# Local attention scores in 64 by 70 blocks instead of 36 by 42, with new settings for the planner that orders the work

## The chip, the cores and the metric

One core of a Trainium2 chip runs the whole program. The metric is the device time of one execution in microseconds, as the median of several runs; lower is better.

## The reference

Input: `q`, `k`, `v` of shape (4 batches, 8 heads, 576 positions, 64), and the weights of two feed-forward layers. Three things follow one another.

1. Attention, twice, for each batch and head. One branch averages `q`, `k` and `v` over groups of 4 positions, runs a full softmax attention over the 144 means, and repeats each result 4 times. The other, the local branch, takes at full resolution only keys with |i - j| < 4, so 7 keys for each query:

```python
mask = np.abs(pos[:, None] - pos[None, :]) < factor      # factor = 4
scores = np.where(mask, scale * np.matmul(q, k.transpose(0, 1, 3, 2)), -1e9)
out_local = np.matmul(softmax(scores), v)
x = (out_up + out_local)       # then (B, H, S, D) -> 2304 tokens x 512
```

2. Layer 1 on the 2304 tokens: `h = x @ w_in` (512 to 2048), `g = max(h, 0) + alpha * min(h, 0)`, `y = g @ w_out` (2048 to 512).
3. Layer 2 of the same sizes with an ELU between its two products.

## The kernel before

**Layer 1** is cut into 128 steps. A step is one group of 288 tokens and one slice `f` of 128 of the 2048 hidden columns: `mm_in` multiplies the tokens by the slice of `w_in`, `th_elem` applies the activation (ScalarE for the part below zero, VectorE for the sum), and, up to two steps later, `out1` multiplies by the slice of `w_out` into four accumulating PSUM banks. There are 8 groups, two to each batch. Operands are split into a high and a low part in the type fp32r, and each product is the sum of three matmuls (high by high, high by low, low by high). ScalarE makes the high part by a copy, VectorE the low part by a subtraction. **The first `F1` steps are different**: they work on the first group's first `F1` slices with unsplit fp32 operands, so that TensorE can start before any split is made; the hardware runs such a matmul as two passes, which appear as two instructions in the trace. Then come the 16 slices of the second group, then the rest of the first, then groups 2 to 7. A weight slice below `F1` is called late: it is decoded first, used unsplit, and split later by `th_late`, which needs one more ScalarE copy than the direct way in `th_conv`.

**Attention** is cut into threads (Python generators) that run beside layer 1. Batch 0 is done in the first 67 us, its local branch by `d_mm` in blocks of 64 queries by 70 keys. Batches 1 to 3 must each be ready before layer 1 reaches their groups at steps 32, 64 and 96. A thread `th_S(b, p)` makes the local scores of one pair of heads: `s_mm` multiplies blocks of 36 queries by 42 keys, `s_ev` copies them out of PSUM (ScalarE), `s_write` stores them to a scratch in DRAM, and `s_read` reads them back by a slanted pattern, 7 scores to a query. In `s_mm` one head lies on rows 0 to 63 of the array (`r = 0`) and the other on rows 64 to 127; the first half of the 576 positions (`c = 0`) goes to PSUM partitions 0 to 63 and the second half (`c = 1`) to those from 64 on, so four matmuls in a row use four different quadrants. `c = 0` is computed 64 queries wide though 36 are kept. Batch 1 makes both heads of its four pairs so, batches 2 and 3 half of theirs: eight `th_S` in all. The other heads of batches 2 and 3 get their scores on VectorE (`s_dve`). The product with the values (`av_ops`) shifts over 7 offsets; for the offsets listed in `AVA` ScalarE does the multiplication (`scale`), for the others VectorE.

**The order of work.** No order is written down by hand. While the program is built, a model of the chip (`_Clock`) keeps a time for each engine, and the order of instructions on each in-order queue comes out of it. A thread yields what it waits for: a key, a buffer token, an engine, or PSUM banks. Between the matmuls of layer 1, `tick` and `fill` let waiting threads emit their work: consumers when the model says that their data are there, TensorE jobs (those that wait for banks) by `pe(budget)` in order of priority until a budget of modelled TensorE time is used up. `PB` is that budget at a tick, `FB` at the start of a step and before `out1`, `RB` while layer 1 itself has to wait. Each thread has a priority (`P1`, `OS`, `OP`, `OSO`, `STEP` and others go into it), some a first step at which they may start (`OPS` for the loads of batches 2 and 3, `ST1` and `ST2` for batch 1), and a limit `LS` on how far ahead of TensorE an engine may be filled. If TensorE would otherwise fall idle, matmuls on a constant tile called `warm` are put in. What the chip then does differently from the model shows as waits in the trace, since the queues keep their order.

Of the kernel before, what the change touches and what calls it, by code (L numbers as in the profile page):

```python
# [7 lines left out]
F32 = mybir.dt.float32  # L8
# [10 lines left out]
S = 576  # L19
D = 64  # L20
NP = H // 2
# [5 lines left out]
NT = 18  # L27
# [1 line left out]
G1 = HT * CH  # L29
NG1 = 2 * B  # L30
NTOK = B * S
BLK = 36
WIN = 7
HALO = 3
KW = BLK + 2 * HALO
NU = 2 * S // BLK
SD = S // 4
TS = 3
LAG = 2
SP_ = S + 2 * HALO  # L40
F1 = 6
VK = 5
YS = 4
LORD = "q0 m q1 v0 d0 q2 v1 d1 q3 v2 d2 v3 d3"
# [2 lines left out]
VP = -15  # L47
DP = -14.5
NP0 = -14.95
STEP = 0.5  # L50
TC = 103
STG = ("n", "gh", "gl", "n", "gh", "gl")
G2 = 512
# [12 lines left out]
ECONV = 100.0  # L66
DLA = 2000.0
PB = 1000.0
FB = 300.0
RB = 300.0  # L70
PF = 5
CS = 6
OS = 4
OP = 13
OPS = -6
OSD = 4
OSO = 0
OAV = 12
OX = -5
UD = -9.5  # L80
# [5 lines left out]
ST2 = 3  # L86
OSS = 0
V1 = 3
LS = 800.0
PM = 300.0  # L90
DMG = 50.0
PM0 = 150.0
DMG0 = 400.0
GATE = "xc", 0, 0
AVA = {1: (2, 4, 6), 2: (2, 4, 6), 3: ()}
SDVE = {1: (), 2: (0,), 3: (0,)}
QUAD = {2, 3}
QORD = 0, 2, 1, 3
# [168 lines left out]
class _Engine:  # L267
# [3 lines left out]
    def cost(self, op, kw, args):  # L271
        if op == "transpose":
            return int(args[1].shape[0]) / 1.2 + 3, int(args[1].shape[0]) * int(args[0].shape[0]) / 16384
        if op == "matmul":
            n, m = _free(kw["out"]), int(kw["out"].shape[0])
            share = int(kw["lhsT"].shape[0]) * m / 16384
            if kw["lhsT"].dtype == BF16:
                return n / 2.4, share
            if kw["lhsT"].dtype == F32R:
                return max(n * 0.4375 + 7, m / 1.2 + 3), share  # L280
            if int(kw["lhsT"].shape[0]) == D and m == BLK:
                return 20.0, share
            if int(kw["lhsT"].shape[0]) == D and int(kw["lhsT"].offset) >= D * int(kw["lhsT"].ap[0][0]):
                return 8.0, share
            if m == D:
                second = int(kw["out"].offset) >= D * int(kw["out"].ap[0][0])
                return 36.0 if second else n * 4 / 2.4 + 16, share
            return n * 4 / 2.4 + 6, share
        sb = (kw["in_"] if "in_" in kw else kw["in0"]).space != bass.MemoryType.PSUM
        if self.name == "ACT":  # L290
            n = _free(kw["out"])
            return (93 if sb else 51) + n / 1.2 + 93.0 * sum(k in kw and not isinstance(kw[k], float) for k in ("scale", "bias")) \
                + (93.0 if "accum_out" in kw else 0.0), None
        n = _free(kw.get("in_", kw["out"]))
        if self.name == "POOL":
            return 150 + n * 2.25, None
        if op == "reciprocal":
            return 68 + n * 6.25, None
        fast = sb and op in ("tensor_scalar", "tensor_copy")
        ptr = op == "scalar_tensor_tensor" and not isinstance(kw["scalar"], (int, float))  # L300
        return 68 + n * (0.52 if fast else 1.0417) + (60 if ptr else 0), None
# [20 lines left out]
def fused_kernel(ctx: ExitStack, tc: tile.TileContext, qk, vt, vl, ql, kl, w_in1, w_out1, alpha,  # L322
# [3 lines left out]
    PE, ACT, DVE, SP, POOL = (_Engine(n, e, ck) for n, e in  # L326
                              (("PE", nc.tensor), ("ACT", nc.scalar), ("DVE", nc.vector), ("SP", nc.sync),
                               ("POOL", nc.gpsimd)))
# [3 lines left out]
    dram = ctx.enter_context(tc.tile_pool(name="dram", bufs=1, space=bass.MemoryType.DRAM))  # L332
# [17 lines left out]
    yT0 = dram.tile([DM, G1], F32, name="yT0a")  # L350
    xsp = dram.tile([128, KT, G1], F32, name="xsp")
    osp = dram.tile([NTOK, DM], F32, name="osp")
    scr = {(b, r): dram.tile([4 * NU // 2, BLK * (KW + 1)], F32, name=f"scr{b}_{r}")
           for b in range(1, B) for r in range(2) if r not in SDVE[b]}

    pB = tc.tile_pool(name="pB", bufs=1)
# [2 lines left out]
    Ap = pA.__enter__()  # L359
# [35 lines left out]

    late = [(1, nm, f) for f in range(F1) for nm in ("i", "o")]

# [183 lines left out]

    def s_mm(b, p, bks):
        t = st["qk", b, p]
        for i in range(NU // 4):
            for c in range(2):
                k = c * (NU // 4) + i
                w = BLK if c else D
                for r in range(2):
                    r0 = r * D
                    PE.matmul(out=bks[r][c * D:c * D + w, i * KW:(i + 1) * KW],  # L590
                              lhsT=t[0][r0:r0 + D, HALO + k * BLK:HALO + k * BLK + w],
                              rhs=t[1][r0:r0 + D, k * BLK:k * BLK + KW], start=True, stop=True)

    def s_ev(bks):
        t = Ap.tile([D + BLK, 2, NU // 4, KW], F32, tag="ss", name="ss", bufs=2)
        for r in range(2):
            ACT.activation(out=t[:, r], in_=bks[r][0:D + BLK, 0:NU // 4 * KW].rearrange("q (u k) -> q u k", k=KW),
                           func=AF.Copy)
        return t

    def s_write(b, p, t):
        for i in range(2):
            u0, r = p * (NU // 2), i
            if b in QUAD:
                u0, r = (2 * p + r - NP) * (NU // 2), 1
            for c in range(2):
                u1 = u0 + c * (NU // 4)
                SP.dma_start(out=scr[b, r][u1:u1 + NU // 4, 0:BLK * KW].rearrange("u (q k) -> q u k", k=KW),
                             in_=t[c * D:c * D + BLK, i])

    def band(t):
        return t.rearrange("u (j t x) -> (u j) t x", t=NT, x=KW + 1)[:, :, 0:WIN]

    def s_read(b):
        for r in (0, 1):
# [195 lines left out]
    T7 = NS1 - NF  # L811
    segs = [(1, 0, 0, F1, 0, 0), (1, 1, 0, NF, 0, 1), (1, 0, F1, NF, 0, 2)]
    segs += [(1, g, 0, NF, g // 2, g % 2) for g in range(2, NG1)]
# [236 lines left out]

    def th_qk(b, p):
        yield "key", "sq", b, p
        if b not in QUAD or p >= NP // 2:
            yield "key", "smm", b, p
        put("qk")

# [101 lines left out]
    def th_soft(b):  # L1158
        yield "key", "sal", b
        for r in range(2):  # L1160
            if r in SDVE[b]:
                for u in range(2):
                    for i in range(HT // TS):
                        yield "key", "SD", b, u, i, r
            else:
                for p in range(NP // 2 if b in QUAD else 0, NP):
                    yield "key", "S", b, p
        yield ("SP",)
        s_read(b)
        yield "tok", "a"  # L1170
        yield ("DVE",)
        softmax_a((b,))
        put("sd")
        yield ("ACT",)
        softmax_e((b,))
        yield ("DVE",)
        softmax_b((b,))
        finish("a", b)
# [230 lines left out]
    def th_elem(s, f):  # L1409
# [3 lines left out]
        n = pool.tile([128, n_], F32, tag="n", name="n", bufs=2)  # L1413
        if s < F1:
            r = pool.tile([128, n_], F32, tag="gh", name="r", bufs=3)
# [7 lines left out]
        finish("h", s)  # L1423
        if s < F1:
            gs[s] = (r, None)
# [11 lines left out]
    def out1(s):  # L1437
# [3 lines left out]
        gh, gl = gs.pop(s)  # L1441
        wk = ("w32" if s < F1 else "w", key)
        run_until(*wk)
# [3 lines left out]
        for m in range(KT):  # L1447
# [3 lines left out]
            at(*t)  # L1451
            if s < F1:
                PE.matmul(out=accb[m][:, :G1], lhsT=W32[key][:, m * 128:(m + 1) * 128], rhs=gh, start=first, stop=last)
# [340 lines left out]
    with tc.manual_schedule():  # L1794
# [4 lines left out]
        for step in LORD.split():  # L1799
            p = int(step[1:] or 0)  # L1800
# [16 lines left out]
        for p in range(NP):  # L1817
            spawn(th_pair(0, p), VP + p * STEP)
            spawn(th_da0(p), DP + p * STEP)
            spawn(th_dense(p, 0), NP0 + p * STEP)  # L1820
            spawn(th_dense(p, 1), US + p / 10, 0)
# [5 lines left out]
        for b in range(1, B):  # L1827
            g0 = 32 * (b - 1)
            for z in range(NP):
                p = QORD[z] if b in QUAD else z  # L1830
                if b not in QUAD or p >= NP // 2:
                    spawn(th_S(b, p), g0 + OS + z if b > 1 else P1 + z / 4)
                spawn(th_qk(b, p), -20)
                spawn(th_pair(b, p), g0 + OP + z if b > 1 else P1 + z / 4, g0 + 2 * z + OPS if b > 1 else ST1 + ST2 * z)
            if b in QUAD:
                for i in range(NP // 2):
                    spawn(th_dav(b, i), g0 + OP + 2 * i + 1)
            spawn(th_sal(b), g0)
            for u in range(2):
                for i in range(HT // TS):  # L1840
                    for r in SDVE[b]:
                        spawn(th_SD(b, u, i, r), g0 + OSD, g0 + OSS, LS)
            spawn(th_soft(b), g0 + OSO, g0)
            for u in range(2):
                spawn(th_vl(b, u), g0 + 5 + u)
                spawn(th_av(b, u), g0 + OAV + 16 * u, -1, LS)
                for i in range(HT // TS):
                    spawn(th_x(b, u, i), g0 + 16 * u + OX + i / 10)
        at(4000.0)
        DVE.tensor_scalar(out=nal, in0=nal, scalar1=-1.0, scalar2=1.0, op0=ALU.mult, op1=ALU.add)  # L1850
        for s in range(NS1):
            slot[0] = s if s else -1
            ly, g, f, first, last, i = seq[s]
# [3 lines left out]
            if s == TC:  # L1857
# [7 lines left out]
                for q in range(NQ):  # L1865
                    p = 2 + max(0, q - NJ + 1) + q / 100
# [13 lines left out]
            if s < F1:  # L1880
                t = 0.0
            else:
                run_until("xc", *segs[i][4:6])
                t = tm["x"]
# [30 lines left out]
        for u in range(NU2):  # L1915
            slot[0] = NS1 + u
            i, j = divmod(u, NJ)
# [106 lines left out]
```

## Time and profile before

| | us |
|---|---|
| median of 3 runs (lowest, highest) | 895.57 (894.94, 895.63) |
| the profiled execution | 896.16 |
| its span, from first to last instruction | 894.1 |
| TensorE matmul busy | 881.1 (99%), 6858 instructions |
| VectorE busy | 740.4 (83%) |
| ScalarE busy | 557.0 (62%) |
| share of TensorE in the chain that ended last | 87% |

A busy TensorE is not one at its peak: matmuls are pipelined, so one of 290 ns begins every 130 ns, and the record of the last before a wait hides a part of that wait. Throughput is therefore read from starts, and idle time from the idle column of a timeline. In timelines the columns are the start, the time from start to end, the engine, the source line, the operation, the tiles (out<-in), their shape and the count, and in brackets the idle time before, with what ended it. All operations pass through one helper, so the source line is the same for all; the tile names tell them apart: `bank<-qk` is `s_mm`, `bank<-qk,qk` is `d_mm`, `x,rawi` and `r,rawo` are the unsplit steps, `xh`, `xl`, `gh`, `gl` with `wi`, `wo` the split ones.

### The profile page before, as it was taken

Reading aid. Unit: us, or ns where it says so; the run is one execution under the profiler, and the core shown is the slowest. Engines: PE = TensorE matmul, PEld = TensorE weight load, DVE = VectorE, ACT = ScalarE, POOL = GpSimd, SP = SyncE. Lnnn points to the kernel's source line nnn. Section 1 sums busy time; section 2 is a strip of 40 time slices with the busy share of each in tenths; the row PEclk is TensorE's granted clock in tenths of the full one; section 3 lists DMA queues with packets and bytes.
Section 4 is the critical chain, followed back from the end, with each engine's and each line's share of the span. In section 5 each row is a group of like instructions: output and inputs, shape, how many; then the busy total and the mean of one; then the engine's idle time right before and its main releaser. Section 6 shows DMA issues by size and latency. Waiting matters only on the chain.

```text
span 894.1 us, 17959 instructions
## 1 busy us (share of the span) xinstructions
PE 881.1 (99%) x6858; PEld 817.1 (91%) x6858; DVE 740.4 (83%) x1600; ACT 557.0 (62%) x1488; POOL 0.2 (0%) x4
## 2 busy tenths in 40 slices
PE   8999999999999999999999999999999999999998
PEld 6678999999998999999999988889999989999987
DVE  5898999999797997997567899888797569888852
ACT  5899887894468844233355676656665457656643
POOL 0000000000000000000000000000000000000000
PEclk9999999999999999999999999999999999999999
DMA  9668733503405032013201733232404063251502
GB/s 293 227 216 284 238 64 108 169 28 101 126 9 169 28 98 57 1 46 111 105 28 59 241 105 121 96 111 79 160 31 164 1 215 117 97 180 33 189 22 73
DMA packets 68310, 102.80 MB, mean 115 GB/s; under 512 B 26704, under 2 KB 43344, under 8 KB 68224
## 3 DMA queue, kind: packets, MB, share of 16 engines
q1 hardware_dynamic: 68224, 101.65, 35.3%
q8 instruction: 54, 0.88, 0.4%
q14 instruction: 32, 0.26, 0.1%
HBM read 84.75 MB, written 16.88 MB: 114 GB/s over the span
## 4 chain that ended last, share of the span: by engine, by line
PE 87%; DVE 4%; ACT 4%; DMA 3%; issue 1%; SPq 0%; DVEq 0%
PE bank L317 87%; ACT n L317 1%; DMA qk<-in_qk_dram 1%; DMA vl<-in_vl_dram 1%; ACT dP L317 1%; DMA rawi<-in_w_in_dram 1%; DMA v<-in_vt_dram 1%; DVE qk L317 0%; ACT P L317 0%; SPq L317 0%; ACT xq L317 0%; DVE P L317 0%; DVE xq L317 0%; ACT gh L317 0%; DVE Dmx L317 0%
## 5 line engine op out<-in xcount | busy, mean ns | idle before, releaser
L317 PE MATMUL bank<-xh,wi 128*128 128x288 f32 x976 | 221.1, 299 | 0.2 <-ACT xh L317 0.2
L317 PE MATMUL bank<-gh,wo 128*128 128x288 f32 x976 | 219.6, 298 | 0.0
L317 PEld LDWEIGHTS bank<-xq,wi 128*128 128x128 f32 x1536 | 194.5, 191 | 6.4 <-DVE xq L317 0.3
L317 PE MATMUL bank<-xq,wi 128*128 128x256 f32 x1536 | 196.6, 283 | 0.1
L317 ACT ACTIVATE n<-bank 128x288 f32<-128x288 f32 (+1 forms) x176 | 70.4, 401 | 180.1 <-PE bank L317 176.7
L317 PE MATMUL bank<-wo,gh 128*128 128x512 f32 x576 | 179.1, 392 | 0.0
L317 PEld LDWEIGHTS bank<-xh,wi 128*128 128x128 f32 x976 | 164.3, 188 | 3.3 <-issue 2.3
L317 PEld LDWEIGHTS bank<-gh,wo 128*128 128x128 f32 x976 | 164.7, 188 | 1.6 <-issue 1.4
L317 PE MATMUL bank<-gl,wo 128*128 128x288 f32 x488 | 144.8, 297 | 0.9 <-DVE gl L317 0.9
L317 PE MATMUL bank<-xl,wi 128*128 128x288 f32 x488 | 143.8, 295 | 0.4 <-DVE xl L317 0.4
L317 PEld LDWEIGHTS bank<-wo,gh 128*128 128x128 f32 x576 | 103.1, 189 | 17.4
L317 PE MATMUL bank<-wo,gl 128*128 128x512 f32 x288 | 112.6, 391 | 0.2 <-DVE gl L317 0.2
L317 PEld LDWEIGHTS bank<-gl,wo 128*128 128x128 f32 x488 | 91.9, 188 | 1.3 <-DVE gl L317 1.3
L317 PEld LDWEIGHTS bank<-xl,wi 128*128 128x128 f32 x488 | 92.0, 189 | 1.0 <-DVE xl L317 0.9
L317 DVE SCALAR_TENSOR_TENSOR r<-n,nal,bank 128x288 f32<-128x288 f32 x128 | 65.1, 509 | 27.4 <-ACT n L317 26.9
L317 ACT ACTIVATE gh<-r 128x288 fp32r<-128x288 f32 x122 | 53.9, 442 | 53.5 <-DVE r L317 53.3
L317 PEld LDWEIGHTS bank<-wo,gl 128*128 128x128 f32 x288 | 54.1, 188 | 13.2 <-DVE gl L317 1.4
L317 DVE TENSOR_TENSOR gl<-r,gh 128x288 fp32r<-128x288 f32 x122 | 55.2, 453 | 11.1 <-ACT gh L317 10.2
L317 ACT ACTIVATE pa<-vl,a 128x64 f32<-128x64 f32 x216 | 55.4, 342 | 0.5 <-DVE a L317 0.5
L317 DVE TENSOR_TENSOR gl<-n,gh 128x512 fp32r<-128x512 f32 (+1 forms) x80 | 50.3, 633 | 6.1 <-ACT gh L317 5.1
L317 DVE TENSOR_TENSOR c<-m,bank 128x256 f32<-128x256 f32 x64 | 26.2, 417 | 33.4 <-PE bank L317 33.2
L317 ACT ACTIVATE gh<-n 128x512 fp32r<-128x512 f32 (+1 forms) x80 | 45.9, 581 | 11.3 <-DVE n L317 11.1
(121 smaller groups left out, 1239.7 us busy)
## 6 DMA issues: line engine op xcount, KB each, us to landing
rawo<-in_w_out_dram SPq DMA_DIRECT2D x38, 512.0 KB
rawi<-in_w_in_dram SPq DMA_DIRECT2D x36, 512.0 KB
qk<-in_qk_dram SPq DMA_DIRECT2D x12, 582.0 KB
vl<-in_vl_dram SPq DMA_DIRECT2D x6, 960.0 KB
x<-yT SPq DMA_DIRECT2D x8, 576.0 KB
osp<-os SPq DMA_DIRECT2D x18, 256.0 KB
os<-osp SPq DMA_DIRECT2D x18, 256.0 KB
out_dram<-os SPq DMA_DIRECT2D x18, 256.0 KB
```

The lines of the kernel that those rows point to most:

```text
L317: return fn(*args, **kw)
```

## The change

The block of local scores becomes 64 queries by 70 keys. 576 positions are 9 such blocks; each column half takes 5, so the middle one is computed in both halves, and the second half writes only its last 4. The settings of the planner are changed along with it, and so is the number of unsplit steps (`F1`, 6 to 8). The model's price of the score matmuls is set anew. Which heads are computed where (`SDVE`) is not changed.

```diff
-BLK = 36
+BLK = 64
-NU = 2 * S // BLK
+NU = S // BLK
+NC = (NU + 1) // 2
-F1 = 6
+F1 = 8
-STEP = 0.5
+STEP = 1.5
-FB = 300.0
-RB = 300.0
+FB = 200.0
+RB = 500.0
-OPS = -6
+OPS = -8
-OSO = 0
+OSO = -2
-LS = 800.0
+LS = 1200.0
-AVA = {1: (2, 4, 6), 2: (2, 4, 6), 3: ()}
+AVA = {1: (2, 4, 6), 2: (3, 5), 3: (3,)}
...
-            if int(kw["lhsT"].shape[0]) == D and m == BLK:
-                return 20.0, share
+            if str(getattr(kw["lhsT"].tensor, "tag", "")).startswith("qk_"):
+                first = [int(kw[k].offset) < D * int(kw[k].ap[0][0]) for k in ("lhsT", "out")]
+                return (98.0 if all(first) else 8.0), share
...
     def s_mm(b, p, bks):
         t = st["qk", b, p]
-        for i in range(NU // 4):
+        for i in range(NC):
             for c in range(2):
-                k = c * (NU // 4) + i
-                w = BLK if c else D
+                k = c * (NU - NC) + i
                 for r in range(2):
                     r0 = r * D
-                    PE.matmul(out=bks[r][c * D:c * D + w, i * KW:(i + 1) * KW],
-                              lhsT=t[0][r0:r0 + D, HALO + k * BLK:HALO + k * BLK + w],
+                    PE.matmul(out=bks[r][c * BLK:(c + 1) * BLK, i * KW:(i + 1) * KW],
+                              lhsT=t[0][r0:r0 + D, HALO + k * BLK:HALO + (k + 1) * BLK],
                               rhs=t[1][r0:r0 + D, k * BLK:k * BLK + KW], start=True, stop=True)
...
     def s_ev(bks):
-        t = Ap.tile([D + BLK, 2, NU // 4, KW], F32, tag="ss", name="ss", bufs=2)
+        t = Ap.tile([2 * BLK, 2, NC, KW], F32, tag="ss", name="ss", bufs=2)
...
     def s_write(b, p, t):
...
             for c in range(2):
-                u1 = u0 + c * (NU // 4)
-                SP.dma_start(out=scr[b, r][u1:u1 + NU // 4, 0:BLK * KW].rearrange("u (q k) -> q u k", k=KW),
-                             in_=t[c * D:c * D + BLK, i])
+                u0 = h * NU + c * NC
+                n = NU - NC if c else NC
+                SP.dma_start(out=scr[b, r][u0:u0 + n, 0:BLK * KW].rearrange("u (q k) -> q u k", k=KW),
+                             in_=t[c * BLK:(c + 1) * BLK, i, NC - n:NC])
```

## Rows read from the trace of the kernel before

**Rows 1.** The page's first part: busy time, share and instructions of each engine.
```profile
PE 881.1 (99%) x6858; PEld 817.1 (91%) x6858; DVE 740.4 (83%) x1600; ACT 557.0 (62%) x1488; POOL 0.2 (0%) x4
```

**Rows 2.** The page's chain that ended last, by engine.
```profile
PE 87%; DVE 4%; ACT 4%; DMA 3%; issue 1%; SPq 0%; DVEq 0%
```

**Rows 3.** Windows, TensorE: stretch, length, busy (instructions), granted clock, DMA share, GB/s.
```profile
0.00:40.00 40.00, 34.34 (x401) 1.00 0.75 255
40.00:70.00 30.00, 30.00 (x260) 1.00 0.76 235
70.00:100.00 30.00, 28.25 (x381) 1.00 0.83 252
100.00:280.00 180.00, 180.00 (x1645) 1.00 0.33 96
280.00:300.00 20.00, 19.18 (x155) 1.00 0.52 201
300.00:890.50 590.50, 589.38 (x4030) 1.00 0.29 95
```

**Rows 4.** Groups by line and shape: the `warm` matmuls (busy us, mean ns).
```profile
L317 PE MATMUL bank<-warm 128*128 128x256 bf16 x84 | 14.6, 309 | 0.9 <-DVE warm L1796 0.9
```

**Rows 5.** Timeline of TensorE around one of the eight score jobs of `s_mm`.
```profile
112.34 0.29 PE L317 MATMUL bank<-gh,wo 128*128 128x288 f32 x1
112.55 1.13 PE L317 MATMUL bank<-qk 64*64 64x42 f32 x64
113.61 0.40 PE L317 MATMUL bank<-gh,wo 128*128 128x288 f32 x1
113.85 0.29 PE L317 MATMUL bank<-gl,wo 128*128 128x288 f32 x1
```

**Rows 6.** Groups by line and shape, TensorE: score matmuls, one form of `s_mm`, and `d_mm`.
```profile
L317 PE MATMUL bank<-qk 64*64 64x42 f32 x256 | 9.0, 229 | 1.8 <-DMA qk<-in_qk_dram 1.4 <-ACT gh L317 0.3
L317 PE MATMUL bank<-qk,qk 64*64 64x70 f32 x160 | 6.8, 229 | 0.6 <-DMA qk<-in_qk_dram 0.6
```

**Rows 7.** Timeline of TensorE: one job of `d_mm` in batch 0.
```profile
8.38 0.83 PE L317 MATMUL bank<-qk,qk 64*64 64x70 f32 x20 [0.30 <-DMA qk<-in_qk_dram]
```

**Rows 8.** Timeline of TensorE: an unsplit run of eight passes, and what follows.
```profile
49.26 2.10 PE L317 MATMUL bank<-x,rawi 128*128 128x288 f32 x8
51.20 0.65 PE L317 MATMUL bank<-r,rawo 128*128 128x288 f32 x2
```

**Rows 9.** Windows, TensorE, a stretch with split matmuls of 288 columns alone.
```profile
425.00:500.00 75.00, 75.00 (x566) 1.00 0.24 79
```

**Rows 10.** Timeline of ScalarE: the extra copy of a late weight slice.
```profile
70.57 0.63 ACT L317 ACTIVATE cw<-rawo 128x512 f32<-128x512 f32 x1 [0.75 <-DVE wi L317]
```

**Rows 11.** Timelines of TensorE: the waits between 40 and 505 us.
```profile
72.91 0.29 PE L317 MATMUL bank<-xh,wi 128*128 128x288 f32 x1
74.64 1.13 PE L317 MATMUL bank<-qk 64*64 64x42 f32 x64 [1.45 <-DMA qk<-in_qk_dram]
...
98.15 0.57 PE L317 MATMUL bank<-qk 64*64 64x42 f32 x29 [0.30 <-ACT gh L317]
...
287.13 0.40 PE L317 MATMUL bank<-gl,wo 128*128 128x288 f32 x1 [0.20 <-DVE gl L317]
...
289.61 0.40 PE L317 MATMUL bank<-xh,wi 128*128 128x288 f32 x1 [0.21 <-ACT xh L317]
290.37 0.40 PE L317 MATMUL bank<-xl,wi 128*128 128x288 f32 x1 [0.36 <-DVE xl L317]
```

**Rows 12.** Timeline of all engines: a reduction by VectorE in the same stretch.
```profile
291.89 1.41 DVE L317 TENSOR_REDUCE sm<-qk 128x144 f32<-128x576 f32 x2
```

**Rows 13.** Groups by line, VectorE: the multiplications of `av_ops`.
```profile
L317 DVE TENSOR_TENSOR pr<-vl,a 128x384 f32<-128x384 f32 x72 | 39.7, 551 | 0.2
```

**Rows 14.** Windows, VectorE, the last 59 us before batch 2 is needed.
```profile
230.00:289.00 59.00, 47.29 (x108) 1.00 0.36 109
```

**Rows 15.** DMA issues: the stores of scores (count, KB each).
```profile
scr<-ss SPq DMA_DIRECT2D x32, 47.2 KB
```

More of the change, by code (lines that the diff above doesn't have):

```diff
@@ L352, in fused_kernel @@
     osp = dram.tile([NTOK, DM], F32, name="osp")
-    scr = {(b, r): dram.tile([4 * NU // 2, BLK * (KW + 1)], F32, name=f"scr{b}_{r}")
+    scr = {(b, r): dram.tile([NP * NU, BLK * (KW + 1)], F32, name=f"scr{b}_{r}")
            for b in range(1, B) for r in range(2) if r not in SDVE[b]}
@@ L583, in s_mm @@
         t = st["qk", b, p]
-        for i in range(NU // 4):
+        for i in range(NC):
             for c in range(2):
-                k = c * (NU // 4) + i
-                w = BLK if c else D
+                k = c * (NU - NC) + i
                 for r in range(2):
                     r0 = r * D
-                    PE.matmul(out=bks[r][c * D:c * D + w, i * KW:(i + 1) * KW],
-                              lhsT=t[0][r0:r0 + D, HALO + k * BLK:HALO + k * BLK + w],
+                    PE.matmul(out=bks[r][c * BLK:(c + 1) * BLK, i * KW:(i + 1) * KW],
+                              lhsT=t[0][r0:r0 + D, HALO + k * BLK:HALO + (k + 1) * BLK],
                               rhs=t[1][r0:r0 + D, k * BLK:k * BLK + KW], start=True, stop=True)
     def s_ev(bks):
-        t = Ap.tile([D + BLK, 2, NU // 4, KW], F32, tag="ss", name="ss", bufs=2)
+        t = Ap.tile([2 * BLK, 2, NC, KW], F32, tag="ss", name="ss", bufs=2)
         for r in range(2):
-            ACT.activation(out=t[:, r], in_=bks[r][0:D + BLK, 0:NU // 4 * KW].rearrange("q (u k) -> q u k", k=KW),
+            ACT.activation(out=t[:, r], in_=bks[r][:, 0:NC * KW].rearrange("q (u k) -> q u k", k=KW),
                            func=AF.Copy)
@@ L602, in s_write @@
         for i in range(2):
-            u0, r = p * (NU // 2), i
+            h, r = p, i
             if b in QUAD:
-                u0, r = (2 * p + r - NP) * (NU // 2), 1
+                r, h = divmod(2 * p + i, NP)
             for c in range(2):
-                u1 = u0 + c * (NU // 4)
-                SP.dma_start(out=scr[b, r][u1:u1 + NU // 4, 0:BLK * KW].rearrange("u (q k) -> q u k", k=KW),
-                             in_=t[c * D:c * D + BLK, i])
+                u0 = h * NU + c * NC
+                n = NU - NC if c else NC
+                SP.dma_start(out=scr[b, r][u0:u0 + n, 0:BLK * KW].rearrange("u (q k) -> q u k", k=KW),
+                             in_=t[c * BLK:(c + 1) * BLK, i, NC - n:NC])
     def band(t):
-        return t.rearrange("u (j t x) -> (u j) t x", t=NT, x=KW + 1)[:, :, 0:WIN]
+        return t.rearrange("u y -> (u y)").rearrange("(j t x) -> j t x", t=NT, x=KW + 1)[:, :, 0:WIN]
     def s_read(b):
@@ L1052, in th_qk @@
         yield "key", "sq", b, p
-        if b not in QUAD or p >= NP // 2:
+        if b not in QUAD or 0 not in SDVE[b] or p >= NP // 2:
             yield "key", "smm", b, p
@@ L1165, in th_soft @@
             else:
-                for p in range(NP // 2 if b in QUAD else 0, NP):
+                for p in range(NP // 2 if b in QUAD and 0 in SDVE[b] else 0, NP):
                     yield "key", "S", b, p
@@ L1830, in fused_kernel @@
                 p = QORD[z] if b in QUAD else z
-                if b not in QUAD or p >= NP // 2:
+                if b not in QUAD or 0 not in SDVE[b] or p >= NP // 2:
                     spawn(th_S(b, p), g0 + OS + z if b > 1 else P1 + z / 4)
```

## Prediction

> **What bounds the kernel now.** I read the page's first part, then its chain, then TensorE in windows, and last the timelines of the places the change touches. TensorE is busy for 881.1 of 894.1 us [rows 1], and the chain that ended last runs through it for 87% [rows 2]. So an edit is worth what it takes from TensorE's instruction stream, plus the waits it ends or starts there; work moved between VectorE and ScalarE counts only through such waits. The windows say where waits can be [rows 3]: 5.7 us idle before 40 us, none from 40 to 70, 1.75 us from 70 to 100, none from 100 to 280, 0.8 us from 280 to 300, and 1.1 us in all after that. In the first 40 us there are besides 14.6 us of `warm` matmuls, which are idle time in disguise [rows 4]. The granted clock is 1.00 throughout, the 2.4 GHz level, and stays out of the sum.
>
> The profiled execution took 896.16 us for a span of 894.1, and the median of the runs is 895.57, 0.59 less. I work out a difference from the profile and put it on the median.
>
> **The score matmuls.** A job of `s_mm` is 32 matmuls in two passes each, 64 instructions; 256 instructions of either form make eight jobs [rows 5, 6]. Around one, the layer's matmul before it starts at 112.34 and the second one after it at 113.85. Without it these two steps would take 2 x 0.1325 us (75 us for 566 matmuls [rows 9]), so a job costs 1.51 - 0.27 = 1.24 us, and eight cost 9.9. Inside, it is busy 1.13 us; less the 0.229 us of its last matmul [rows 5, 6], 0.90 us lie between first and last start. The 64 passes come in 16 steps of four quadrants, so a step takes 0.90 / 15.5 = 58 ns. The other 0.3 us are entry and exit, which stay.
>
> After, a job is 5 block pairs by 2 heads by 2 halves = 20 matmuls, 40 passes, 10 steps. A step with 70 keys and weights 64 wide in all four quadrants does not occur before. The nearest row is `d_mm`, with the same block on two quadrants: 20 passes of 0.229 us, busy 0.83 us [rows 6, 7], so 0.60 us for 10 pairs less the last half step: 61 to 63 ns a pair. I take 61, as the 58 of now shows that four quadrants run beside one another. The job then saves 16 x 58 - 10 x 61 = 318 ns, and eight save **2.5 us**, all of it on TensorE. The lower bound keeps the 58 ns: 6 x 58 x 8 = 2.8 us saved. In the upper one the two column halves of a head take turns, so a step is 122 ns: 10 x 122 - 928 = 292 ns more, and eight jobs cost 2.3 us more than now.
>
> A rule of the Trainium skill speaks for the upper bound: "TensorE: Matmul & The Clock Gate", in "Part 3: Packing small matmuls — row/col tiling", lets a weight load overlap running matmuls only where the row group differs, and the two halves of one head share theirs. By that rule the sum gets 4.8 us worse. In this trace the two halves already share a row group, with weights 64 and 36 wide, and the step is 58 ns, less than one full block pair of `d_mm` needs on its own [rows 5 to 7]; so the measurement is against it here, though not yet for two full halves.
>
> **Around the score matmuls.** `s_ev` copies 350 columns instead of 336 on ScalarE, which isn't the bound. The stores stay 32 [rows 15] with the same number of strips, each 70 floats instead of 42, so two thirds more on 32 x 47.2 KB = 1.5 MB, with SP issuing as often. None of TensorE's waits after 40 us is for either [rows 11]: the split matmuls of layer 1 hide them, and I cost both at nothing. If that cover were gone, 14 more columns of 350 and two thirds more bytes would make a softmax late by well under 1 us (an estimate from these counts).
>
> **F1 from 6 to 8.** Two slices of the first group, 2 x (4 + 4) = 16 products, go from three split matmuls to one unsplit in two passes. Eight passes take 51.20 - 49.26 = 1.94 us [rows 8], so a product is 485 ns against 3 x 132.5 = 397.5 [rows 9]. That adds 16 x 87.5 ns = **1.4 us**, in a stretch where TensorE has no idle time to hide it [rows 3]. In return every split weight is due some 16 x 0.485 = 7.8 us later. Four more slices pass through the late way, one ScalarE copy of 0.63 us each [rows 10], 2.5 us against those 7.8, so ScalarE gains slack. The only wait it could end is the 0.30 us before 98.15 [rows 11]. Bounds: 1.1 to 1.4 us more.
>
> **The planner's settings.** `STEP` does nothing: with 0.5 as with 1.5 the threads of pair p all stand before those of pair p + 1 (at 0.5 two priorities are equal, and the earlier spawned goes first), and none passes another group. So the first 40 us stay as they are, but for `RB`. `FB` and `RB` decide how many jobs are put in at one place; one merged or split job is worth the 0.3 us of entry and exit. I take 0, within 0.6 either way.
>
> `OPS`, `OSO`, `LS` and `AVA` change what lies on VectorE and ScalarE, and so only the waits. Between 40 and 505 us they are 1.45 us for the first block of `q` and `k` of batch 1, then 0.30, and 0.20 + 0.21 + 0.36 around 288 us [rows 11]: 2.5 us idle. Counted from starts it is about 0.16 us more for each of the five (72.91 to 74.64 us is 1.73 against 0.13), so 3.3. The ones near 288 us stand at the entry into batch 2's first group, where a 1.4 us pair of reductions for batch 3 shares VectorE with the splits [rows 11, 12]. `OPS` = -8 lets batch 3's loads start two steps earlier, so these reductions fall before the entry. `AVA` moves one of three offsets of batch 2 from ScalarE to VectorE, six multiplications of 0.551 us = 3.3 us [rows 13], into a stretch in which VectorE has 59 - 47.3 = 11.7 us free [rows 14]; it fits. The wait for batch 1's load stays: the load is issued by the same rule at step 6, into the same busy DMA stretch (0.83 from 70 to 100 us [rows 3]). What is late next there is the same job of `s_mm`. I take 1.2 us of the 3.3 as saved. Bounds: 3.3 saved, or as much added.
>
> Nothing else is touched: after 505 us there is only layer 2.
>
> **Sum.** -2.5 + 1.4 + 0 - 1.2 = -2.3 us: the profile goes from 896.16 to 893.9, and the median from 895.57 to **893.3 us**. About 0.2%, or 1.8 us, is what a measurement of this kernel can tell from no change.
>
> **The rivals.**
>
> *Waits stay.* The new order has as many waits as the old, in other places: -2.5 + 1.4 = -1.1, 894.5 us. For it: most of the wait time is one DMA wait that no setting addresses. Against it: the ones around 288 us have a cause that `OPS` moves.
>
> *All waits go.* -2.5 + 1.4 - 3.3 = -4.4, 891.2 us. Against it: the model has to be right on a load that it missed by 1.45 us before.
>
> *Slower, score jobs queued ahead of their data.* TensorE's queue is in order, so a job that the model puts in too early holds back all of layer 1 behind it. Place: the four score jobs of batch 1, between 62 and 115 us, loaded while weights stream. Price: what the first one lost, 1.73 - 0.13 = 1.6 us each [rows 11]. It decides from the point where new waits outweigh the -1.1: one more makes +0.5, two more +2.1, 897.7 us. For it: two more jobs of the unsplit part now run past step 6, in which the loads start. Against it: the other three jobs of batch 1 waited 0.3 us together.
>
> *Slower, halves take turns.* The upper bound of the step: +2.3 + 1.4 = +3.7, 899.3 us, with the waits as they are. Against it stands the 58 ns.
>
> *The change does less than it says* for `STEP` only.
>
> **Chances.** Forecast 0.48, waits stay 0.27, all waits go 0.07, score jobs too early 0.13, halves take turns 0.05. The forecast spreads about 1 us to either side, so it gives 0.44 faster and 0.04 same; waits that stay give 0.23 same, 0.03 faster, 0.01 slower; too early 0.02 same, 0.11 slower. Faster 0.54, same 0.29, slower 0.17. The range goes from 890.8, which takes in all waits gone and the lower bound of the step, to 897.0, which takes in one more early job and leaves out most of the two slower cases. The likeliest case alone spans 892.3 to 894.3.
>
> **What would show it.** The new score jobs with 40 passes, busy 0.80 us in place of 1.13 (1.4 us and more if the halves take turns). Sixty-four instead of 48 passes of `x,rawi` and of `r,rawo`. A first 40 us like the old, with the same `warm` count within a few. Near 290 us waits under 0.3 us together, and before the first score job of batch 1 still one on `qk`. I am wrong if the idle time from 70 to 300 us grows beyond the 2.6 of now, if the start-up changes by more than 1 us, or if the step isn't near 61 ns.

## The result, and the profile after

The changed kernel takes 900.06 us (median of 8 runs, 897.73 to 902.35) where the kernel before took 895.6 on the same chip (8 runs, 893.64 to 898.24): a ratio of 1.0054 [1.0037, 1.0071]. It is slower; 893.3 was forecast, and 900.06 lies above the range. The profiled execution took 900.28 us, 4.1 more than the 896.16 of before, for a span of 898.5 (4.4 more).

The page's first part and its chain of the kernel after, to be read against [rows 1, 2]:
```profile
PE 882.1 (98%) x6650; PEld 816.5 (91%) x6650; DVE 739.7 (82%) x1598; ACT 559.2 (62%) x1490; POOL 0.2 (0%) x4
...
PE 83%; DVE 6%; ACT 4%; DMA 4%; issue 1%; SPq 1%; DVEq 0%; ACTq 0%
```
TensorE has 208 instructions fewer and is busy 1.0 us longer, and its share of the chain fell from 87% to 83%. The windows of TensorE after (columns and stretches of [rows 3]) say where:
```profile
0.00:40.00 40.00, 34.35 (x403) 1.00 0.74 259
40.00:70.00 30.00, 30.00 (x241) 1.00 0.75 250
70.00:100.00 30.00, 26.92 (x265) 1.00 0.69 211
100.00:280.00 180.00, 177.17 (x1544) 0.98 0.37 104
280.00:300.00 20.00, 19.46 (x196) 1.00 0.56 180
300.00:510.00 210.00, 210.00 (x1608) 1.00 0.22 71
```
The first 70 us are as before. From 70 to 280 us TensorE is idle 5.9 us where it was idle 1.75, and the clock is no longer 1.00 throughout. The timeline of TensorE after shows three things in that stretch: a score job in its new form (91.48), and the two waits that hold most of the idle time:
```profile
82.93 0.29 PE L319 MATMUL bank<-xh,wi 128*128 128x288 f32 x1
85.48 0.40 PE L319 MATMUL bank<-xh,wi 128*128 128x288 f32 x1 [2.26 <-DVE r L319]
...
91.26 0.29 PE L319 MATMUL bank<-xh,wi 128*128 128x288 f32 x1
91.48 0.85 PE L319 MATMUL bank<-qk 64*64 64x70 f32 x40
92.26 0.40 PE L319 MATMUL bank<-xh,wi 128*128 128x288 f32 x1
92.50 0.29 PE L319 MATMUL bank<-xl,wi 128*128 128x288 f32 x1
...
98.89 0.29 PE L319 MATMUL bank<-xh,wi 128*128 128x288 f32 x1
102.19 1.44 PE L319 MATMUL bank<-qk 64*64 64x70 f32 x40 [3.01 <-DMA qk<-in_qk_dram]
103.57 0.61 PE L319 MATMUL bank<-xh,wi 128*128 128x288 f32 x1
103.97 0.44 PE L319 MATMUL bank<-xl,wi 128*128 128x288 f32 x1
104.21 0.68 PE L319 MATMUL bank<-xh,wi 128*128 128x288 f32 x2
```
The undisturbed job runs from 91.26 to 92.50 with its neighbours: 1.24 us from the start of the matmul before it to that of the second after it, against 112.34 to 113.85 = 1.51 [rows 5]. The third job of batch 1 waits for its `q` and `k`. From the starts, 98.89 to 102.19 is 3.30 us against a usual 0.13: 3.2 us lost; the other wait is 85.48 - 82.93 less 0.13, 2.4 us lost. Behind the second, matmuls start 0.24 us apart (103.97, 104.21) in place of 0.13. Windows of TensorE after, columns as before:
```profile
102.00:103.00 1.00, 0.81 (x28) 0.50 0.62 252
103.00:105.00 2.00, 2.00 (x30) 0.50 0.05 20
105.00:107.00 2.00, 2.00 (x10) 0.50 0.46 102
...
108.00:109.00 1.00, 1.00 (x10) 1.00 0.30 54
```
The granted clock is 0.50, the 1.2 GHz level, from 101.1 to 107.9 us. Before it fell, TensorE had stood idle since the end of its last matmul at 99.2 us. Of the eight runs the one with a mean granted clock of 1.000 took 897.73 us, the other seven, at 0.992 to 0.997, took 899.72 to 902.35.

Why the data were late is on SP, which issues the DMAs in order. Its timeline after (start, time to issue, what is moved, count):
```profile
87.28 2.12 SPq L319 DMA_DIRECT2D yT0a<-ys  x4
92.88 3.18 SPq L319 DMA_DIRECT2D scr<-ss  x4
96.11 0.61 SPq L319 DMA_DIRECT2D qk<-in_qk_dram  x1
```
and at the same place before:
```profile
90.16 1.72 SPq L317 DMA_DIRECT2D scr<-ss  x4
91.98 0.37 SPq L317 DMA_DIRECT2D qk<-in_qk_dram  x1
```
The four score stores of the job before stand ahead of the load that the next job waits for. They cannot start until the scores are out of PSUM: SP, free at 89.40 us (87.28 + 2.12, stores of another tile), stands for them until 92.88. Then they take 3.18 us of SP where they took 1.72.

SP stood for its stores in the kernel before too, where the second job, whose scores they move, starts here:
```profile
87.67 1.13 PE L317 MATMUL bank<-qk 64*64 64x42 f32 x64
```
Counted from the start of the second job, the load for the third is issued after 4.31 us before (91.98) and after 4.63 us now (96.11). But TensorE comes to the third job 10.2 us behind the second before (98.15 less the wait of 0.30 [rows 11]) and 7.7 us behind it now (99.18). From the load's issue to the job it is 6.08 us now and 6.17 before, so the load itself is no slower. Two things meet: a load that leaves no earlier, because the stores hold SP longer, and a new order that asks for it 2.5 us sooner. The experiments on block and order tell what each is worth.

Each store alone, as the views of the tile `scr` in the traces before and after have it (min/median/max ns to issue):
```profile
L317 SPq DMA_DIRECT2D scr<-ss x32: 318/414/1577, 76.3 to 343.8; - x32
```
```profile
L319 SPq DMA_DIRECT2D scr<-ss x32: 574/612/1490, 71.2 to 293.7; - x32
```
Still 32 stores, but 64 partitions instead of 36 in each, and 612 ns to issue instead of 414.

### The profile page after: what moved, and what is told of

The parts are those of the page before. It is cut to its first block, busy times and chain, and to the rows that moved or that the text cites. A ratio compares the mean times of both kernels' runs of the same rounds, so it can differ in the third digit from the quotient of the medians.

```text
span 898.5 us, 17535 instructions
## 1 busy us (share of the span) xinstructions
PE 882.1 (98%) x6650; PEld 816.5 (91%) x6650; DVE 739.7 (82%) x1598; ACT 559.2 (62%) x1490; POOL 0.2 (0%) x4
## 4 chain that ended last, share of the span: by engine, by line
PE 83%; DVE 6%; ACT 4%; DMA 4%; issue 1%; SPq 1%; DVEq 0%; ACTq 0%
PE bank L319 83%; DMA rawi<-in_w_in_dram 2%; DMA qk<-in_qk_dram 1%; ACT n L319 1%; DVE acc L319 1%; ACT P L319 1%; SPq L319 1%; DVE sm L319 1%; DMA v<-in_vt_dram 1%; ACT dP L319 1%; DVE x L319 1%; DVE gl L319 0%; DVE qk L319 0%; DVE pr L319 0%; DVE r L319 0%
## 5 line engine op out<-in xcount | busy, mean ns | idle before, releaser
L319 PE MATMUL bank<-xh,wi 128*128 128x288 f32 x960 | 216.5, 299 | 2.3 <-DVE r L319 2.3
L319 PEld LDWEIGHTS bank<-xh,wi 128*128 128x128 f32 x960 | 162.2, 189 | 4.8 <-DVE r L319 2.5
L319 PEld LDWEIGHTS bank<-gh,wo 128*128 128x128 f32 x960 | 162.7, 189 | 2.1 <-issue 1.8
L319 PE MATMUL bank<-gl,wo 128*128 128x288 f32 x480 | 142.0, 296 | 0.4 <-DVE gl L319 0.4
```

Of the source, the lines that this page charges most:

```text
L319: return fn(*args, **kw)
```

## Experiments

All were timed against the kernel before on their own chip (893.77 us for the first four, 895.03 for the next four, 894.99 for the last four). Letters in the expectations are theories; the two that were left in the end are H, the stores' place in SP's in-order queue, and T, the transfers of the larger stores themselves. Lost time, where it is told, is what the starts of TensorE's matmuls between 40 and 900 us show beyond the usual distance, summed over gaps of at least 0.3 us: 4.6 us in the kernel before, 7.7 after.

### The block alone, and the settings alone

`block_only` is the change without its settings:
```diff
-F1 = 8
+F1 = 6
...
-AVA = {1: (2, 4, 6), 2: (3, 5), 3: (3,)}
+AVA = {1: (2, 4, 6), 2: (2, 4, 6), 3: ()}
```


> The new block and its price in the planner, with all settings of before. Theory Q (what was lost is a wait: the load of q and k for batch 1's third score job is issued late, behind the stores of the second one, and TensorE stands 3.0 us before that job and then runs 5.7 us at the lower clock): eight jobs at 0.28 us less, so -2.2 us, and new waits only where a load is late; 892.5 to 896. Rival P (the blocks themselves cost TensorE more than worked out): slower than before, 896 to 899. Rival O (any new order of this planner loses as much): also 897 or more.

904.13 us (902.99 to 906.98), ratio 1.011 [1.0095, 1.0124]: worse than the whole change, so the settings are not what made it slow. Theory Q's 892.5 to 896 was missed, and by its number alone rival O would do as well. TensorE and SP in its trace, around the second score job of batch 1:
```profile
81.69 0.29 PE L319 MATMUL bank<-xh,wi 128*128 128x288 f32 x1
85.19 0.85 PE L319 MATMUL bank<-qk 64*64 64x70 f32 x40 [3.21 <-DMA qk<-in_qk_dram]
```
```profile
75.51 3.77 SPq L319 DMA_DIRECT2D scr<-ss  x4
79.32 0.61 SPq L319 DMA_DIRECT2D qk<-in_qk_dram  x1
```
The same picture one job earlier: stores, then the load, then a job that stands 3.2 us. In all 12.2 us are lost, some 7 of them elsewhere (133, 178 to 182, 298 to 301 us), where another order of work has other waits, and the granted clock falls to the 1.2 GHz level three times, for 3.4 us each.

`settings_only` is the kernel before with the eight settings of the change:

> The new settings with the old blocks of 36 by 42. Q: +1.9 us for the two more unsplit steps, the old price of the score jobs, and waits that depend on whether the new order puts a score job ahead of its load; without such a wait 896.5 to 898.5. P: the settings are not the cause, 895 to 897. O: 899 or more, with long waits before 120 us.

895.35 us (894.46 to 897.1), ratio 1.0016 [1.0008, 1.0025]; lost time 2.5 us, and no wait of 1 us after the first 40. The settings cost 1.6 us, which is about what `F1` was to cost. This speaks against rival O: here a new order alone brings no long wait. That the 2.1 us of lost time that this trace has less than the one before do not show in the median stays open.

### One load, and a guard for the clock

`load_first` is the changed kernel with one edit on SP: the load for the third job of batch 1 goes out ahead of the stores of the second. In part, with a comment added:
```diff
+    LATER = {(1, 1)}
...
         SP.dma_start(out=t, in_=qk[b, p])
         st["qk", b, p] = [t[:, 0], t[:, 1]]
+        flush()          # issues the stores kept back by s_write for LATER
```


> The changed kernel; only on SP's queue the load of q and k for batch 1's third pair is issued ahead of the four score stores of the second pair, all other engines keep their order. Q: the load is issued near 92.9 instead of 96.1 us, the wait before the third job falls from 3.0 to under 0.5 us, the clock stays at 1.00, and 3.0 + 2.6 us come back: 894 to 896. If the load isn't late because of the queue but because the transfers are slow: the wait shrinks by less than 1.5 us, 897.5 to 900. P and O: 899 to 901.

897.61 us (895.19 to 899.53), ratio 1.0041 [1.0027, 1.0054]: less came back than Q forecast. The load is issued at 89.59 us and the wait before the third job is gone; the one near 83 us stays, now with a fall of the clock behind it (86.2 to 89.6 us), and the next late load is the fourth job's, behind the third job's stores and two weight loads:
```profile
115.02 0.85 PE L319 MATMUL bank<-qk 64*64 64x70 f32 x40 [2.18 <-DMA qk<-in_qk_dram]
```
So the late loads are not tied to one place: moving one uncovers the next.

`warm_guard` puts 30 matmuls on the constant tile `warm` ahead of the third job, to keep TensorE from standing idle there; their results are not used.
```diff
+        if (b, p) == (1, 2):
+            for _ in range(30):
+                nc.tensor.matmul(out=bks[0][:, 0:256], lhsT=warm[:, 0:1].to_broadcast([128, 128]), ...)
```


> The changed kernel with 30 matmuls on the constant tile put straight ahead of batch 1's third score job, some 3.3 us that take the place of the idle time. Q: the job starts at the same time or 0.3 us later, the granted clock stays at 1.00, and what comes back is the clock alone: 897 to 898, 2.6 us less than the changed kernel. If the lower clock cost nothing: 900 to 900.5.

899.11 us (896.09 to 902.35), ratio 1.0061 [1.0041, 1.0081]. Inconclusive: in its profile the wait near 83 us was the one behind which the clock fell, and the guard stands behind that. The price of the clock by itself was not measured by an experiment; the rows give it: in the kernel after a split matmul takes 0.24 us for 0.13 over some 5.7 us, about 2.6 us, and the one run with a clock of 1.000, 2.5 us below the profiled one, is in line with it.

### Block and order apart

`block_old_order` computes the new blocks in the order of the kernel before, instruction by instruction on every engine, by showing the planner the old shapes (the edit in short, with comments added):
```diff
+                    kw = {"out": ..., "lhsT": ..., "rhs": ...}        # 36 by 42
+                    ck.op("PE", *PE.cost("matmul", kw, ()), ...)      # the model's clock alone
+        for i in range(ML):                                           # and the blocks of 64 by 70
+                    nc.tensor.matmul(out=bks[r][c * BL:(c + 1) * BL, i * KL:(i + 1) * KL], ...)
```


> The new blocks in the order of before: the planner is fed with the old block's shapes, so every engine has the queue of before, and only the eight score jobs, their copies and their stores are the new ones. Theory Q2 (the new block is worth its 0.28 us a job; what was lost is the new order, in which TensorE's jobs stand ahead of data that come late): 1.5 to 2.5 us less than before, no new wait over 0.5 us. Rival S (the stores, 64 rows at 0.6 us of issue instead of 36 at 0.4, hold up the loads behind them in any order): new waits of 1 us and more before the second to fourth score job, 1 us less to 1 us more than before.

894.88 us (892.79 to 895.57), ratio 0.9987 [0.9975, 0.9999]. TensorE's waits for `q` and `k` in the score jobs (in all, times, longest, us):
```profile
PE bank L603 <- DMA qk<-in_qk_dram: 1.3, 3, 0.6
```
So neither expectation holds: the waits of 1 us and more of rival S did not come, nor did Q2's 1.5 to 2.5 us. `old_block_new_order` is the reverse: the order of the changed kernel with blocks of 36 by 42, their copies and stores.

> The counterpart: the order of the changed kernel, with the old blocks, copies and stores put into it. Q2: the waits stay for the most part (2.3 us at 83 us, 1.5 to 3 us before a score job of batch 1) and the lower clock may come with them: 4.5 to 7 us more than before. S: without the long stores the waits shrink under 1 us in all; left are the two more unsplit steps: 2 to 3 us more than before.

896.89 us (895.38 to 899.71), ratio 1.0018 [1.0007, 1.003]. The block by itself is worth -0.13%, the order by itself +0.18%, and the two together +0.54%: the rest, some 4 us, is neither's own. The lost time of the four traces, one execution each, says the same: 4.6 us before, 6.2 with the new blocks in the old order, 3.2 with the old blocks in the new order, 7.7 with both. So the new blocks, with their copies and stores, add 1.6 us of waits in the old order and 4.5 in the new one, where the clock falls besides.

Its place shows in the last trace. With the old stores the load for the third job is issued at 93.38 us in place of 96.11, the job waits 1.40 us in place of 3.01, and the clock stays at 1.00:
```profile
93.38 0.41 SPq L320 DMA_DIRECT2D qk<-in_qk_dram  x1
```
```profile
99.22 1.41 DVE L320 TENSOR_REDUCE sm<-qk 128x144 f32<-128x576 f32 x2 [1.25 <-DMA qk<-in_qk_dram]
99.34 1.13 PE L603 MATMUL bank<-qk 64*64 64x42 f32 x64 [1.40 <-ACT P L320]
```
The view puts this wait down to ScalarE's `P`, which came last. But VectorE stood for the same load until 99.22 us, so without `P` the job could have started hardly earlier: here too the load is late.

### The stores out of the way, and in the way

`stores_behind` keeps back the stores of the first three pairs of batch 1 until the next pair's load has been issued, on SP as before (the edit is told against `load_first`):
```diff
-    LATER = {(1, 1)}
+    LATER = {(1, 0), (1, 1), (1, 2)}
```


> The changed kernel; on SP alone, the score stores of batch 1's first three pairs wait until the load of the next pair has been issued. Q2: the load waits before the second to fourth job fall under 0.5 us together; the wait at 83 us behind a late weight load goes too if the first pair's stores held that load up, else it stays at 2.3: 0 to 1 us more than before, or 2 to 3.5 with that wait. If transfers and not the queue are slow: as the changed kernel, 4 to 5 us more than before.

893.3 us (891.56 to 894.17), ratio 0.9974 [0.9962, 0.9985]: faster than the kernel before, where Q2 had given no gain. From 70 to 100 us TensorE is busy again:
```profile
70.00:100.00 30.00, 29.79 (x322) 1.00 0.80 237
```
Both long waits are gone, the one near 83 us too, which `load_first` still had: the two differ only in where the stores of the first and third pair stand. What is left is 1.3 us lost before the second job of batch 2, whose stores are where they were.

`stores_twice` takes the kernel before, with its old blocks and its order, and issues each store of scores a second time, to a scratch that nobody reads:
```diff
+                nc.sync.dma_start(out=scr2[u1:u1 + NU // 4, 0:BLK * KW].rearrange("u (q k) -> q u k", k=KW),
+                                  in_=t[c * D:c * D + BLK, i])
```


> The kernel before, with each score store issued a second time into a scratch that nobody reads: twice the issue time on SP and twice the transfer, more than the new block adds. Q2: that order has room, 0 to 1 us more than before. S: loads come 1.7 us later, 2 to 5 us more than before.

906.72 us (905.5 to 907.74), ratio 1.0124 [1.0108, 1.014]. TensorE's waits for `q` and `k` (in all, times, longest, us), and the job with the longest:
```profile
PE bank L317 <- DMA qk<-in_qk_dram: 5.2, 3, 2.4
```
```profile
88.24 1.94 PE L317 MATMUL bank<-qk 64*64 64x42 f32 x64 [2.41 <-DMA qk<-in_qk_dram]
```
So more stores alone bring waits of this kind into a kernel that had one, and the clock falls at two of them. But the second store doubles both the issue time and the transfer, so H and T are not yet apart.

`stores_pool` does that. It is the changed kernel, everything in its order, with the 32 stores issued from GpSimd's queue, where nothing else waits. The transfers stay; SP is rid of them.
```diff
-                SP.dma_start(out=scr[b, r][u0:u0 + n, 0:BLK * KW].rearrange("u (q k) -> q u k", k=KW),
-                             in_=t[c * BLK:(c + 1) * BLK, i, NC - n:NC])
+                o = scr[b, r][u0:u0 + n, 0:BLK * KW].rearrange("u (q k) -> q u k", k=KW)
+                ck.dma(o, t[c * BLK:(c + 1) * BLK, i, NC - n:NC])
+                nc.gpsimd.dma_start(out=o, in_=t[c * BLK:(c + 1) * BLK, i, NC - n:NC])
```


> The changed kernel; all 32 score stores are issued by GpSimd's queue instead of SP's, the transfers and all other orders stay. Theory H (what holds the loads up is SP's queue: the loads stand in it behind stores that wait for ScalarE's copy and take 0.6 us each to issue): the load waits in batch 1 and the one at 83 us go, 1 to 3 us less than before. Rival T (the stores' transfers, 1.6 us of all DMA engines a job, crowd out the loads): the waits stay, 3 to 5 us more than before.

891.34 us (890.13 to 891.76), ratio 0.9955 [0.9942, 0.9968]: the fastest kernel of the case, 8.7 us under the changed one by their medians (8.1 when each is set against the kernel before on its own chip), and better than the 1 to 3 us that H gave. Its tile `scr`, TensorE's windows, and the timelines of GpSimd, of SP, where the load for the third job stands, and of TensorE at that job:
```profile
L612 POOL DMA_DIRECT2D scr<-ss x32: 630/661/792, 72.1 to 286.1; - x32
```
```profile
70.00:100.00 30.00, 29.99 (x321) 1.00 0.88 304
100.00:280.00 180.00, 180.00 (x1559) 1.00 0.35 105
```
```profile
91.62 1.98 POOL L612 DMA_DIRECT2D scr<-ss  x3 [15.73 <-ACT ss L319]
```
```profile
87.44 0.45 SPq L319 DMA_DIRECT2D qk<-in_qk_dram  x1
```
```profile
97.48 0.85 PE L319 MATMUL bank<-qk 64*64 64x70 f32 x40
```
A store takes about as long to issue as on SP (661 ns) and moves the same bytes. But now the stores wait for ScalarE's `ss` in a queue of their own, and the load for the third job goes out at 87.44 us in place of 96.11, the one for the fourth at 91.40 in place of 109.49. TensorE loses 0.9 us from 40 us on, and the clock is 1.00. H holds; by T the waits would have stayed, all the more as the DMA engines are busier from 70 to 100 us than in the changed kernel (0.88 against 0.69). The transfers are not quite the same: they go in 1536 packets where they took 9728. But `stores_behind`, which leaves the packets and the queue as they were, gains as well, so the gain doesn't need the other packets.

The trace explains the wait near 83 us too. It ended with `r` on VectorE, which needs `n` from ScalarE, whose queue stood for weights. ScalarE after, and with the stores on GpSimd's queue:
```profile
80.23 0.68 ACT L319 ACTIVATE cp<-rawo 128x512 f32<-128x512 f32 x1 [2.59 <-DMA rawo<-in_w_out_dram]
...
84.49 0.39 ACT L319 ACTIVATE n<-bank 128x288 f32<-128x288 f32 x1
```
```profile
78.85 0.67 ACT L319 ACTIVATE cp<-rawo 128x512 f32<-128x512 f32 x1 [0.59 <-DMA rawo<-in_w_out_dram]
...
82.86 0.38 ACT L319 ACTIVATE n<-bank 128x288 f32<-128x288 f32 x1
```
In the kernel after four weight loads stand on SP behind the first job's four stores (71.22 to 73.89 us), which themselves stand for their data. With the stores on GpSimd's queue these four go out 0.8 to 1.0 us earlier, and `n` comes 1.6 us earlier. So the stores held up weights and scores alike.

The Trainium skill sets little on such a move: "DMA: Bandwidth & Descriptors", in "Issuing engines are not separate DMA queues", says that issuing from several engines saves only the sequencer's time, "usually small relative to the DMA itself". Here the saved sequencer time is 32 x 0.612 = 20 us of SP over 890, small indeed; what it was worth lay in the loads behind it, which the trace shows leaving 8.7 us earlier at the third job.

### The same with the old order, and all stores behind

`old_order_behind` and `old_order_pool` are `block_old_order` with the edits of `stores_behind` and of `stores_pool`.

> The new blocks in the order of before, with batch 1's stores behind the next load on SP. That order has no two more unsplit steps (1.9 us less than the new one), but some 3 us of waits between 251 and 291 us that loads don't cause. H: the load waits of 1.8 us before the first three score jobs shrink under 0.8 us: 2 to 3.5 us less than before. T: as without it, about 1 us less than before.

> The new blocks in the order of before, with all score stores on GpSimd's queue. H: 2 to 4 us less than before. T: about 1 us less than before.

892.67 us (891.71 to 893.56), ratio 0.9971 [0.9961, 0.9982], and 891.92 us (890.05 to 894.56), ratio 0.9965 [0.9952, 0.9979]. The old order gains too, by 2.2 and 3.0 us on its own 894.88; once the stores are out of the way the two orders differ by less than their intervals.

`behind_all` was meant to better `stores_behind`: the stores of batches 2 and 3 are kept back too, until the next load of `q` and `k` or the reading back (the edit is told against `stores_behind`).
```diff
-    LATER = {(1, 0), (1, 1), (1, 2)}
+    LATER = {(b, p) for b in range(1, B) for p in range(NP)}
...
     def s_read(b):
+        flush()
```


> As the kernel that put batch 1's stores behind the next load, which took 0.26% less than before; now also those of batches 2 and 3. H: the load wait of 1.3 us at 164 us that was left there goes too: 2.5 to 4 us less than before. T: no change against that kernel, 2 to 2.6 us less than before.

911.15 us (910.39 to 912.61), ratio 1.0182 [1.0169, 1.0195]: a miss, by the same kind of error as the prediction's. VectorE's wait for the operands of its own scores (in all, times, longest, us), a row of its timeline, and one of SP's:
```profile
DVE spr L319 <- DMA qls<-in_ql_dram: 21.2, 10, 2.6
```
```profile
223.44 0.62 DVE L319 TENSOR_TENSOR spr<-kls,qls 128x448 f32<-128x448 f32 x1 [2.33 <-DMA qls<-in_ql_dram]
```
```profile
234.96 2.57 SPq L608 DMA_DIRECT2D scr<-ss  x4
```
Batch 2's last scores, ready before 170 us, are stored at 235 us, and `ss` has two buffers, which it shares with `kls`, the keys of the heads that VectorE computes. With one buffer held, the next keys are loaded only when the last have been used; VectorE stands 21.2 us, layer 1's `r` and `gl` stand behind it, and TensorE waits 8.3 us for `gl` and 5.0 for `r`. That the buffer is the cause was read from the code and these rows; no run gave `kls` one of its own.

## Why the prediction was wrong

**What bounds the kernel** was read rightly: the time went where TensorE's idle time went.

**The score matmuls** were right. A job costs 1.24 us less the 0.27 of its two neighbours, against 1.51 less the same: 0.27 us saved, 2.2 us in eight, where 318 ns and 2.5 were forecast. The 40 passes are there; their first and last start lie 0.63 us apart, so a step is 0.63 / 9.5 = 66 ns instead of 61. The halves do not take turns, and the trace disagrees with the rule that the prediction took from "TensorE: Matmul & The Clock Gate" of the Trainium skill: with two full halves in one row group a step is 66 ns, not 122.

**F1** was nearly right. Counted from starts the added passes take 8.25 us and replace 16 x 397.5 ns = 6.36: 1.9 us more where 1.4 was forecast. The median of `settings_only`, +1.6 us, agrees.

**The planner's settings**: the waits near 288 us went, though one of 0.54 us at 285.9 came, and the 1.45 us before the first job of batch 1, which I held to stay, went too. By `settings_only` the settings were no cost beyond `F1`: its lost time is 2.1 us less than before, where I took 1.2 as saved. What I did not see is that the new order leaves 2.5 us less between the second and the third score job. That `STEP` does nothing was not tested by itself.

**Around the score matmuls** is the step that failed. "The stores stay 32", "with SP issuing as often", "I cost both at nothing". I counted the stores and their bytes and took the DMA share to be their price, hidden by layer 1. Their price is SP's: 64 partitions take 612 ns to issue and 36 took 414, so a job's four stores hold SP some 0.8 us longer by the medians and 1.5 us longer ahead of the third job's load; and before that they hold it until ScalarE has copied the scores, 3.5 us there. Every load behind waits as long. What I put at nothing measured 1.6 us of waits in the old order, and 4.5 us and a fall of the clock in the new one. [Rows 11] had shown none of TensorE's waits as a store's, but a store never appears there: it appears as the DMA of the load behind it. The 1.45 us for `qk` in the kernel before, though no store stood ahead of that load, was the sign to look at SP's queue, which I did not.

It is the rival "score jobs queued ahead of their data", given 0.13, that came true, in the place it named, and with it the sign of being wrong: the idle time from 70 to 300 us grew from 2.6 to 6.5 us. Its price was too low: 1.6 us for one job, where the third lost 3.2 and a second wait, by way of ScalarE, 2.4; and I kept the clock out of the sum, which fell inside the longer wait.

**The sum**, measured: -2.2 (score jobs), +1.9 (`F1`), +3.1 (waits, 4.6 to 7.7 us), +2.6 (clock) = +5.4 against the +4.4 of the span; 1 us isn't accounted for. With the stores on GpSimd's queue: -2.2 + 1.9 - 3.7 (waits, 4.6 to 0.9) = -4.0 against -4.5. By the medians the change gains 1.7 us with three pairs' stores behind the loads and 3.7 with all stores on GpSimd's queue: the forecast's 2.3 lies between, so it is what the change is worth about when the stores cost nothing.

**Open.** Why the planner puts the loads where it does was only read, not tried: it charges a transfer twice in pieces under 256 bytes, and the strips grew from 168 to 280, so it prices the new stores lower, while it books one fixed time for the issue of any DMA. The waits of `block_only` after 130 us were not followed up.

## What to carry to other kernels

In this kernel a DMA's price had three parts: its bytes, the time its queue needs to issue it, and the time the queue stands until its data are ready; the last two were paid by the loads behind it, and the profile books them as waits for those loads. Before costing a changed store at nothing, read the issuing queue's timeline, see which load stands behind it and how long the order leaves until that load is needed, and put stores that wait for compute on another queue, or behind the next load, but only as long as no buffer is held that others need. Where a wait grows, add what the clock does after it.

## What the hardware showed

- A store of scores took 414 ns to issue from 36 partitions and 612 ns from 64, both on SP (medians of 32), and 661 ns from 64 on GpSimd's queue.
- The granted clock fell to the 1.2 GHz level at 101.1 us, inside a 3.0 us idle stretch of TensorE, and was back at 107.9, though TensorE worked from 102.2 on; a split matmul took 0.24 us for 0.13. In `old_block_new_order`, with a wait of 1.40 us at that place, it stayed at 2.4 GHz.
- Four quadrants with weights 64 wide and 70 columns each take 66 ns a step, where two quadrants of the same block take 61 to 63 [rows 7].
